# A fused attention and two-layer MLP kernel: all attention scores as float32 matmuls, with the two halves of the features in two row tiles of TensorE

## The chip, the cores and the metric

The kernel runs on one core of a Trainium2 chip, as one launch. The metric is the device time of one execution in microseconds. The engines are named as in the profile: PE is the matrix engine (its weight loads are listed apart, as PEld), DVE the vector engine, ACT the scalar engine, POOL is hardly used here, and SP issues the DMAs.

## The reference

Attention over 4 batches, 8 heads, 768 tokens and 64 features a head, in chunks of 32 tokens that see 16 tokens to the left, 8 to the right and 8 memory tokens; then two layers of an MLP, 512 to 2048 to 512, over all 3072 tokens.

```python
for c in range(nc):                      # 24 chunks of 32 tokens
    l_start = max(0, c_start - left_ctx)
    r_end = min(S, c_end + right_ctx)
    k_full = np.concatenate([mem_k, k[:, :, l_start:r_end]], axis=2)
    v_full = np.concatenate([mem_v, v[:, :, l_start:r_end]], axis=2)
    scores = scale * np.matmul(q_c, k_full.transpose(0, 1, 3, 2))
    scores = scores - np.max(scores, axis=-1, keepdims=True)
    a = np.exp(scores)
    a = a / (np.sum(a, axis=-1, keepdims=True) + 1e-09)
    out[:, :, c_start:c_end] = np.matmul(a, v_full)
...
h = x @ w_in                             # layer 1
x = (h * np.clip(h + 3.0, 0.0, 6.0) / 6.0) @ w_out
...
h = x @ w_in                             # layer 2
g = np.where(h >= 1, h, np.where(h <= -1, 0.0, (h + 1) ** 2 / 4.0))
x = g @ w_out
```

## The kernel before

**Attention.** The tokens are cut into 32 blocks of 96 queries (`QB`) and 128 keys (`KB`). A block has two halves of four heads (`GRP`): half 0 has its 64 features a head on partitions 0 to 63, half 1 on 64 to 127. Each call of `group(j, half, key)` does one half of block `j`: scores (tile `sc`), a maximum over keys, `exps` on ACT (tile `st`), `weigh` and `norm` on DVE, `turn` (four transposes on PE into `tp`), a copy `pt` on ACT or DVE, `values` (four matmuls on PE into `pv`, heads in turn on output partitions 0 to 63 and 64 to 127), and `x_high`/`x_low`, which write the result as a sum of two rounded parts into the MLP's input tiles `xhi` and `xlo`.

**Two kinds of scores.** The first ten blocks (`NEARLY`) are "early": PE adds the mask with one bfloat16 matmul (L373) and the four heads' scores with float32 matmuls on 64 rows (L379). The other 22 blocks are "late": the loads bring each half's q and k twice, to both halves of the partitions; ACT and DVE split q and k into a rounded part and the rest (`qs` L407 and L415, `ks` L410 and L417); PE makes the scores with `fp32r` matmuls on all 128 rows (L424, two of 256 columns a run, two runs a half); and DVE adds the mask and the two parts in two steps (L430, L436).

**MLP.** `xbuf` holds 6 tiles `n` of 512 tokens a layer. For each of 16 slices `f` of the hidden features (step `k` counts them over both layers, 192 in all) PE makes `ph` (12 matmuls, L526 to L528), ACT and DVE the activation and its two parts `ghi` and `glo`, and PE adds 12 matmuls into four PSUM tiles `py` (layer 1, L575 to L577) or `po` (layer 2, L580 to L582). After 16 slices ACT or DVE copy them out to `ysb` or `osb` and SP stores them. Layer 2 loads layer 1's result back as `x2raw`. The weights come packed and are unpacked by ACT and DVE (`raw`, `w`), once a layer.

**What sets the order.** `Plan.run` is a list scheduler that runs when the program is built. Each task has an engine (or two to choose from), an estimated duration, a key (a due time in steps of `k`) and buffers; a buffer takes a slot of a pool when its first task starts, and gives it back after the last. Each engine's instructions are emitted in the order of planned starts, so on the chip every engine works through a fixed list. The pools of interest: PSUM banks `a` (2; scores, `tp` and `pv` of attention), `y` (4) and `h` (2); places `o` (2) for results to be stored, `in` (2) for q and k, `lv` (3) for v, `st` (2), `pt` (1). In the first blocks some of these may also take `w` or `y` slots. Where PE would stand idle in the first 60 us of the plan, matmuls on a zero tile `warm` are put in (L687).

Blocks 0 to 5 feed the first tile `n = 0` and come ahead of the MLP; block order is all first halves, then all second halves. The other blocks are spread over the MLP steps of layer 1 by their keys.

Of the kernel before, what the change touches and what calls it, by code (L numbers as in the profile page):

```python
# [75 lines left out]
class Plan:  # L76
# [41 lines left out]
    def slot_for(self, b):  # L118

        found = []  # L120
        for p in b.pools:
            free = [s for s in self.pools[p] if not s.used]
            if len(free) > b.keep.get(p, 0):
                found.append(min(free, key=lambda s: s.at))
        return min(found, key=lambda s: s.at) if found else None

    def run(self, at):
# [13 lines left out]
        while left:  # L141
            best = None
            for e, ts in ready.items():
                found = []
                blocked = set()
                for t in sorted(ts, key=lambda t: (t.key, t.n)) if e == "SP" else ts:
                    est = max(free[e], t.ready)
                    for b in t.bufs:
                        if b.slot is None:
                            s = None if blocked & set(b.pools) else self.slot_for(b)  # L150
                            if s is None:
                                est = None
                                break
                            est = max(est, s.at + HOP)
                    if est is None and e == "SP":

                        blocked.update(p for b in t.bufs if b.slot is None for p in b.pools)
                    if est is not None:
                        found.append((est, t))
# [18 lines left out]
            if t.kb:  # L178
                bw = max(bw, t.end + 1500) + t.kb / 0.39
                t.end = bw  # L180
            for b in t.bufs:
                if b.slot is None:
                    b.slot = self.slot_for(b)
                    b.slot.used = True
# [31 lines left out]
def fused_kernel(ctx: ExitStack, tc: tile.TileContext, qkv, qk, vv, wpk, const, out):  # L216
# [4 lines left out]
        "w": NSLOT, "xhi": 2, "xlo": 2, "r": 2, "ghi": 3, "glo": 3, "st": 2, "pt": 1, "xt": 1,  # L221
        "o": 2, "in": 2, "lv": 3, "qs": 1, "ks": 1, "sm": 4,
# [107 lines left out]
    q_buf, v_buf = {}, {}  # L330

    def early_load(j, key):
        q = q_buf[j] = Buf(["w", "in"], [128, NP * (QB + KB)], F32, "q_sb", w=1)
        v = v_buf[j] = Buf(["w", "in"], [128, H * D], F32, "v_sb", w=1)
        o = NP * (QB + KB)
        add(("SP", 400), key - 6, lambda e: nc.sync.dma_start(tile_of(q), qkv[j, :, :o]), writes=[(q, 0)], kb=448)
        add(("SP", 400), key - 4, lambda e: nc.sync.dma_start(tile_of(v), qkv[j, :, o:]), writes=[(v, 0)], kb=256)

    def group(j, half, key):
        early = j < NEARLY  # L340
        first = key < 0
        bank = ["a", "y"] if first else ["a"]
        spare = ["w"] if first else []
        st = Buf(["st"] + spare, [128, GRP, KB], F32, "st", w=4)
        sm = Buf(["sm"], [128, 4, GRP], F32, "sm")
        pt = Buf(["pt"] + spare, [128, GRP, QB], F32, "pt", w=4)
        tp = Buf(bank, [128, GRP, QB], F32, "tp")
        pv = Buf(bank, [128, 2, QB], F32, "pv")
        small = lambda i: tile_of(sm)[:QB, i]

        def exps(src, n):
            s = tile_of(st)[:QB]
            for i in range(n):
                A.activation(
                    out=s[:, i, :], in_=src[:, i, :], func=AF.Exp, scale=scale,
                    bias=small(2)[:, i:i + 1], accum_out=small(0)[:, i:i + 1],
                )

        def peak(e, src):
            V.tensor_reduce(out=small(1), in_=src(), axis=AX.X, op=ALU.max)  # L360

        def negate(e):
            V.tensor_scalar(out=small(2), in0=small(1), scalar1=-scale, scalar2=None, op0=ALU.mult)

        if early:
            sc = Buf(bank, [128, GRP, KB], F32, "sc", a=1)
            q = q_buf[j]

            def scores(e):
                t, c = tile_of(q), tile_of(sc)  # L370
                q3 = t[:, :NP * QB].rearrange("p (a t) -> p a t", a=NP)
                k3 = t[:, NP * QB:].rearrange("p (a t) -> p a t", a=NP)
                P.matmul(  # L373
                    c[:QB], cbf[:QB, 3 * KB:3 * KB + QB], mask_of(j, GRP),
                    start=True, stop=False, skip_group_check=True,
                )
                hp = 64 * half
                for i in range(GRP):
                    P.matmul(  # L379
                        c[:QB, i, :], q3[hp:hp + 64, i, :], k3[hp:hp + 64, i, :],  # L380
                        start=False, stop=True, skip_group_check=True,
                    )

            add(("PE", 1350), key - 4, scores, [(q, 0), "cbf"], [(sc, 0)], hold=[st], line="scores")
            src, at = lambda: tile_of(sc)[:QB], (sc, 0)
            add(("DVE", dve(512, psum=True)), key - 3.5, lambda e: peak(e, src), [at], [(sm, 1)])
            add(("DVE", 90), key - 3.4, negate, [(sm, 1)], [(sm, 2)])
            add(("ACT", 1420), key - 3, lambda e: exps(src(), GRP), [at, (sm, 2)], [(st, 0), (sm, 0)])
        else:

            over = key > 1.75 * NF
            x = Buf(["in", "w"] if over else ["in"], [128, LATE_W], F32, "late_sb")
            xv = Buf(["lv"], [128, GRP * D], F32, "late_v")
            qs = Buf(["qs"], [128, GRP, QB], F32R, "qs")
            ks = Buf(["ks"], [128, GRP, 2, KB], F32R, "ks")
            g = 2 * (j - NEARLY) + half
            q3 = lambda: tile_of(x)[:, :GRP * QB].rearrange("p (a t) -> p a t", a=GRP)
            k3 = lambda: tile_of(x)[:, GRP * QB:LATE_W].rearrange("p (a t) -> p a t", a=GRP)

            def load(e, hp):  # L400
                nc.sync.dma_start(tile_of(x)[hp:hp + 64], qk[g])

            def load_v(e):
                nc.sync.dma_start(tile_of(xv), vv[g])
# [7 lines left out]
            add(("SP", 350), key - 9, lambda e: load(e, 0), writes=[(x, 0)], kb=224, after=last_w if over else (), line="load")  # L412
# [345 lines left out]
```

## Time and profile before

| | us |
|---|---|
| median of 3 runs (lowest, highest) | 1214.09 (1213.93, 1215.21) |
| the profiled execution: its time | 1214.17 |
| the profiled execution: span from the first to the last instruction | 1212.4 |
| PE busy in the span | 1194.1 |
| DVE busy | 747.5 |
| ACT busy | 555.1 |

The span is what the views of the trace divide up; 1.8 us of the execution's time lie around it. Matmuls are pipelined, and the profile's duration of one is longer than the distance to the next: how long a matmul takes of PE's time is read from the distance between starts. A float32 matmul is recorded as two instructions (a run of four matmuls is listed as x8).

### The profile page before, as it was taken

The numbers are of one execution on the slowest core, as the hardware profiler recorded it, in microseconds if no ns is written. First come the engines' busy times: TensorE is split into PE (matmuls) and PEld (weight loads), VectorE is DVE, ScalarE is ACT, GpSimd is POOL, SyncE is SP. The second block draws the span as 40 slices with busy tenths as digits, with TensorE's granted clock in tenths as the row PEclk, the third lists the DMA queues.
The fourth block names the chain that finished last, engine by engine and source line by source line (L and its number), as shares of the span: only waits on it lengthen the run. The fifth ranks groups of instructions, "written<-read, shape, count | busy, mean of one in ns | idle before, by whom it ended". The sixth has DMA issues, their size and how long they took to land.

```text
span 1212.4 us, 15631 instructions
## 1 busy us (share of the span) xinstructions
PE 1194.1 (98%) x5811; PEld 956.7 (79%) x5811; DVE 747.5 (62%) x1427; ACT 555.1 (46%) x1323; POOL 0.2 (0%) x4
## 2 busy tenths in 40 slices
PE   9999999999999999999999899999999999999998
PEld 6677777777777777777888688888888888888886
DVE  4999988768766764873598843533533533533433
ACT  4988656546545544653477722322222322322221
POOL 0000000000000000000000000000000000000000
PEclk9999999999999999999999999999999999999999
DMA  9615124223221320320255610200200200000000
GB/s 366 264 62 156 51 73 111 59 60 109 64 60 53 100 59 25 109 60 21 88 181 184 193 34 1 71 1 1 70 1 1 70 1 1 35 1 1 35 1 35
DMA packets 36060, 86.74 MB, mean 72 GB/s; under 512 B 4624, under 2 KB 10384, under 8 KB 35984
## 3 DMA queue, kind: packets, MB, share of 16 engines
q1 hardware_dynamic: 35984, 85.74, 22.2%
q8 instruction: 46, 0.75, 0.3%
q14 instruction: 30, 0.25, 0.1%
HBM read 73.14 MB, written 12.58 MB: 71 GB/s over the span
## 4 chain that ended last, share of the span: by engine, by line
PE 79%; DVE 10%; ACT 5%; DMA 4%; issue 1%; SPq 0%; ACTq 0%; DVEq 0%
PE ph L526 12%; PE ph L527 12%; PE ph L528 12%; PE po L580 7%; PE po L581 7%; PE po L582 7%; PE py L575 5%; PE py L576 5%; PE py L577 5%; DMA raw<-wpk 2%; PE pv L467 2%; PE sc L379 1%; PE tp L457 1%; PE sc L424 1%; DVE raw L297 1%
## 5 line engine op out<-in xcount | busy, mean ns | idle before, releaser
L526 PE MATMUL ph<-xhi,w 128*128 128x512 f32 x768 | 303.9, 396 | 0.3 <-DVE r L552 0.3
L527 PE MATMUL ph<-xlo,w 128*128 128x512 f32 x768 | 299.5, 390 | 0.0
L528 PE MATMUL ph<-xhi,w 128*128 128x512 f32 x768 | 299.4, 390 | 0.0
L549 ACT ACTIVATE r<-r,bias 128x512 f32<-128x512 f32 x96 | 69.4, 723 | 288.3 <-DVE r L546 288.3
L556 DVE TENSOR_TENSOR glo<-r,ghi 128x512 fp32r<-128x512 f32 x192 | 132.2, 689 | 81.3 <-ACT ghi L555 80.2
L555 ACT CAST ghi<-r 128x512 fp32r<-128x512 f32 x192 | 119.3, 622 | 116.6 <-DVE r L552 71.6
L526 PEld LDWEIGHTS ph<-xhi,w 128*128 128x128 f32 x768 | 144.2, 188 | 31.3 <-DVE r L552 0.7
L528 PEld LDWEIGHTS ph<-xhi,w 128*128 128x128 f32 x768 | 144.2, 188 | 30.9
L527 PEld LDWEIGHTS ph<-xlo,w 128*128 128x128 f32 x768 | 144.3, 188 | 27.7
L546 DVE TENSOR_SCALAR r<-ph 128x512 f32<-128x512 f32 x96 | 66.3, 691 | 148.3 <-PE ph L528 148.3
L575 PE MATMUL py<-ghi,w 128*128 128x512 f32 x384 | 157.2, 409 | 0.5 <-ACT ysb L597 0.4
L580 PE MATMUL po<-w,ghi 128*128 128x512 f32 x384 | 149.7, 390 | 4.3 <-DVE ysb L601 2.3
L576 PE MATMUL py<-glo,w 128*128 128x512 f32 x384 | 150.4, 392 | 0.0
L577 PE MATMUL py<-ghi,w 128*128 128x512 f32 x384 | 150.2, 391 | 0.0
L581 PE MATMUL po<-w,ghi 128*128 128x512 f32 x384 | 149.4, 389 | 0.0
L582 PE MATMUL po<-w,glo 128*128 128x512 f32 x384 | 149.4, 389 | 0.0
L552 DVE TENSOR_TENSOR r<-ph,r 128x512 f32<-128x512 f32 x96 | 66.3, 691 | 75.9 <-ACT r L549 75.9
L539 ACT ACTIVATE r<-ph,bias 128x512 f32<-128x512 f32 x96 | 65.7, 684 | 90.3 <-PE ph L528 78.9
L542 DVE SCALAR_TENSOR_TENSOR r<-r,ph 128x512 f32<-128x512 f32 x96 | 65.4, 681 | 46.8 <-ACT r L539 46.0
L580 PEld LDWEIGHTS po<-w,ghi 128*128 128x128 f32 x384 | 72.0, 188 | 20.4 <-ACT ysb L597 2.9
L575 PEld LDWEIGHTS py<-ghi,w 128*128 128x128 f32 x384 | 72.1, 188 | 17.2 <-ACT ysb L597 1.4
L577 PEld LDWEIGHTS py<-ghi,w 128*128 128x128 f32 x384 | 72.1, 188 | 16.2
(66 smaller groups left out, 1331.2 us busy)
## 6 DMA issues: line engine op xcount, KB each, us to landing
raw<-wpk SPq DMA_DIRECT2D x64, 512.0 KB, 4.3
late_sb<-qk SPq DMA_DIRECT2D x88, 224.0 KB, 3.5
ymid<-ysb SPq DMA_DIRECT2D x24, 256.0 KB, 2.9
x2raw<-ymid SPq DMA_DIRECT2D x24, 256.0 KB, 4.3
out<-osb SPq DMA_DIRECT2D x24, 256.0 KB, 2.0
late_v<-vv SPq DMA_DIRECT2D x44, 128.0 KB, 2.1
q_sb<-qkv SPq DMA_DIRECT2D x10, 448.0 KB, 7.0
v_sb<-qkv SPq DMA_DIRECT2D x10, 256.0 KB, 6.8
```

What stands on the lines that cost most here:

```text
L526: P.matmul(p, whi[:, c, :], xh[:, c, :], start=(c == 0), stop=False)
L527: P.matmul(p, whi[:, c, :], xl[:, c, :], start=False, stop=False)
L528: P.matmul(p, wlo[:, c, :], xh[:, c, :], start=False, stop=(c == NC - 1))
L549: add(("ACT", act(T) + 100), k + 0.35, lambda e: A.activation(out=rt(), in_=rt(), func=AF.Square, bias=bias[:, 1:2], scale=0.5,), [], [(r, ...
L555: add(("ACT", act(T)), k + 0.5, lambda e: A.copy(tile_of(ghi), rt()), [(r, 0)], [(ghi, 0)])
L556: add(("DVE", dve(T)), k + 0.6, lambda e: V.tensor_tensor(out=tile_of(glo), in0=rt(), in1=tile_of(ghi), op=ALU.subtract,), [(r, 0), (ghi, ...
L575: P.matmul(y, w2hi, gh, start=first, stop=False)
L576: P.matmul(y, w2hi, gl, start=False, stop=False)
L577: P.matmul(y, w2lo, gh, start=False, stop=last)
L580: P.matmul(y, gh[:, t], wt[:, 0], start=first, stop=False)
L581: P.matmul(y, gh[:, t], wt[:, 1], start=False, stop=False)
L582: P.matmul(y, gl[:, t], wt[:, 0], start=False, stop=last)
```

## The change

- The block's two halves are one task on PE: `scores` of a block alternates between half 0 (rows 0 to 63 of the array) and half 1 (rows 64 to 127), each with its own PSUM bank. From block 6 on (from the second tile on) both halves' `turn` is one run of eight transposes, and both halves' `values` one run of eight matmuls.
- All blocks use the float32 scores. Early blocks keep the mask by PE; for the late ones DVE adds the mask in one step of 512 columns. The splits of q and k, and their second loads, are gone.
- Keys: the first tile's blocks come block by block (both halves next to each other) rather than half by half.
- Pools: `st` 3, `pt` 2, `lv` 2 (of twice the width), `qs` and `ks` gone. Results to be stored may also take `st` and `in` places in layer 2 and for the last tile of layer 1.
- The planner reckons 1900 rather than 1500 ns for a DMA's latency, takes all slots of a task at once, and fills 1300 ns more with `warm` matmuls ahead of the first real one.

```diff
-        "w": NSLOT, "xhi": 2, "xlo": 2, "r": 2, "ghi": 3, "glo": 3, "st": 2, "pt": 1, "xt": 1,
-        "o": 2, "in": 2, "lv": 3, "qs": 1, "ks": 1, "sm": 4,
+        "w": NSLOT, "xhi": 2, "xlo": 2, "r": 2, "ghi": 3, "glo": 3, "st": 3, "pt": 2, "xt": 1,
+        "o": 2, "in": 2, "lv": 2, "sm": 4,
...
+        for half in range(2):
+            g, p, c = 2 * (j - NEARLY) + half, slice(64 * half, 64 * half + 64), slice(256 * half, 256 * half + 256)
+            add(
+                ("SP", 350), key - 9, lambda e, g=g, p=p: nc.sync.dma_start(tile_of(q)[p], qk[g]),
+                writes=[(q, half)], kb=224, after=last_w if over else (), line="load",
+            )
...
-            def q_low(e):
-                V.tensor_tensor(out=tile_of(qs)[64:], in0=q3()[64:], in1=tile_of(qs)[64:], op=ALU.subtract)
-
-            def k_low(e):
-                V.tensor_tensor(out=tile_of(ks)[:, :, 1], in0=k3(), in1=tile_of(ks)[:, :, 0], op=ALU.subtract)
...
+            for i in range(GRP):
+                for h in half:
+                    P.matmul(
+                        tile_of(sc[h])[:QB, i, :], q3[64 * h:64 * h + 64, i, :], k3[64 * h:64 * h + 64, i, :],
+                        start=not by_pe and i == 0, stop=True, skip_group_check=True,
                     )
...
+            def mask(e):
+                V.tensor_tensor(out=s(), in0=tile_of(sc[h])[:QB], in1=mask_of(j, GRP), op=ALU.add)
...
+        add(
+            ("PE", 1200 + 460 * by_pe), keys[0] - 4, scores, [(q, 0), (q, 1), "cbf"],
+            [(sc[0], 0), (sc[1], 0)], hold=st, line="scores",
+        )
...
+            add(
+                ("PE", 710), keys[1] - 2, lambda e: [turn(h) for h in half], [(st[0], 0), (st[1], 0), "ident"],
+                [(tp[0], 0), (tp[1], 0)], hold=pt, line="turn",
+            )
...
-                o = Buf(["o"], [128, T], F32, "osb" if l else "ysb")
+
+                o = Buf(["o", "st", "in"] if l or n == NT - 1 else ["o"], [128, T], F32, "osb" if l else "ysb")
...
-                    while at + ns <= t.start:
+                    while at + ns <= t.start + more:
```

Three places show how the instructions move.

PE, between two MLP steps of layer 1, with a late block under way. Before (`sc` are a half's scores, `ph` and `py` the MLP's):

```order
L528 MATMUL ph<-xhi,w 128x512
L424 MATMUL sc<-ks,qs 96x256 x2
L575 MATMUL py<-ghi,w 128x512
L576 MATMUL py<-glo,w 128x512
L577 MATMUL py<-ghi,w 128x512
L575 MATMUL py<-ghi,w 128x512
L576 MATMUL py<-glo,w 128x512
L577 MATMUL py<-ghi,w 128x512
L424 MATMUL sc<-ks,qs 96x256 x2
```

and of the change (`tp` are the transposes of one block, `sc` the scores of the next):

```order
L520 MATMUL ph<-xhi,w 128x512
L393 MATMUL tp<-ident,st 128x96 x8
L567 MATMUL py<-ghi,w 128x512
L568 MATMUL py<-glo,w 128x512
L569 MATMUL py<-ghi,w 128x512
L567 MATMUL py<-ghi,w 128x512
L568 MATMUL py<-glo,w 128x512
L569 MATMUL py<-ghi,w 128x512
L386 MATMUL sc<-q_sb 96x128 x8
L567 MATMUL py<-ghi,w 128x512
```

Eight short runs of attention a block (four of scores, two of transposes, two of values) have become three longer ones, and six MLP matmuls stand between a block's transposes and the next block's scores.

PE at the start of the program, behind the first `warm` matmuls. Before, one half of blocks 0, 1 and 2:

```order
L373 LDWEIGHTS cbf
L373 MATMUL sc<-cbf 96x512
L379 MATMUL sc<-q_sb 96x128 x4
L373 LDWEIGHTS cbf
L373 MATMUL sc<-cbf 96x512
L379 MATMUL sc<-q_sb 96x128 x4
L687 LDWEIGHTS warm
L687 MATMUL sc<-warm 128x512
```

and of the change, both halves of block 0, and the masks of block 1:

```order
L379 LDWEIGHTS cbf
L379 MATMUL sc<-cbf 96x512
L379 LDWEIGHTS cbf
L379 MATMUL sc<-cbf 96x512
L386 MATMUL sc<-q_sb 96x128 x8
L379 LDWEIGHTS cbf
L379 MATMUL sc<-cbf 96x512
```

Both masks now go ahead of the block's eight float32 matmuls.

ACT where layer 2 begins, around the copies `ysb` of layer 1's last tile (`xhi<-x2raw` is layer 2's second input tile). Before:

```order
L555 CAST ghi<-r 128x512
L252 CAST xhi<-x2raw 128x512 x3
L252 CAST w<-raw 128x512
L281 ACTIVATE raw<-raw 128x512
L549 ACTIVATE r<-r,bias 128x512
L287 ACTIVATE raw<-raw 128x512
L555 CAST ghi<-r 128x512
L597 ACTIVATE ysb<-py 128x512 x2
```

and of the change:

```order
L547 CAST ghi<-r 128x512
L253 CAST w<-raw 128x512
L253 CAST xhi<-x2raw 128x512 x3
L253 CAST w<-raw 128x512
L590 ACTIVATE ysb<-py 128x512
L541 ACTIVATE r<-r,bias 128x512
L282 ACTIVATE raw<-raw 128x512
L590 ACTIVATE ysb<-py 128x512
```

ACT's first copy stands nearer behind the three casts of `x2raw`; the casts still stand ahead of it.

## Rows read from the trace of the kernel before

**Rows 1.** The page: busy us of each engine, share of the span, instructions.
```profile
PE 1194.1 (98%) x5811; PEld 956.7 (79%) x5811; DVE 747.5 (62%) x1427; ACT 555.1 (46%) x1323; POOL 0.2 (0%) x4
```

**Rows 2.** Windows: stretch, us, busy us (count) of PE, PEld, DVE, ACT, POOL; clock, DMA.
```profile
10.00:20.00 10.00, 10.00 (x42) 7.01 (x42) 5.94 (x17) 2.98 (x16) 0.00 (x0) 1.00 1.03 409
20.00:30.00 10.00, 10.00 (x76) 7.78 (x75) 6.84 (x19) 6.91 (x31) 0.00 (x0) 1.00 1.02 404
...
60.00:100.00 40.00, 39.33 (x218) 29.67 (x216) 37.84 (x74) 32.08 (x79) 0.00 (x0) 1.00 0.31 106
...
200.00:550.00 350.00, 347.61 (x1831) 274.12 (x1830) 246.92 (x547) 182.75 (x531) 0.00 (x0) 1.00 0.26 71
...
650.00:700.00 50.00, 45.35 (x197) 36.33 (x196) 44.53 (x72) 37.18 (x62) 0.00 (x0) 1.00 0.58 189
```

**Rows 3.** Windows of the instructions on tile w alone: PE's are the MLP matmuls.
```profile
200.00:550.00 350.00, 318.43 (x1269) 228.89 (x1268) 0.00 (x0) 0.00 (x0) 1.00 0.26 71
700.00:1200.00 500.00, 500.00 (x2208) 414.02 (x2207) 0.68 (x1) 0.00 (x0) 1.00 0.05 18
```

**Rows 4.** Timeline of PE in layer 1: start us, us, instruction.
```profile
255.65 0.40 PE L424 MATMUL sc<-ks,qs 128*96 128x256 f32 x2
255.88 0.39 PE L575 MATMUL py<-ghi,w 128*128 128x512 f32 x1
...
258.65 0.39 PE L577 MATMUL py<-ghi,w 128*128 128x512 f32 x1
258.96 0.55 PE L467 MATMUL pv<-pt,late_v 128*64 128x96 f32 x8
259.45 0.50 PE L526 MATMUL ph<-xhi,w 128*128 128x512 f32 x1
259.79 0.40 PE L527 MATMUL ph<-xlo,w 128*128 128x512 f32 x1
```

**Rows 5.** Timeline of PE in the first 60 us.
```profile
17.77 2.02 PE L379 MATMUL sc<-q_sb 64*96 64x128 f32 x8
19.72 1.54 PE L467 MATMUL pv<-pt,v_sb 128*64 128x96 f32 x16
21.20 0.90 PE L457 MATMUL tp<-ident,st 96*128 96x96 f32 x4
...
24.41 0.91 PE L467 MATMUL pv<-pt,v_sb 128*64 128x96 f32 x8
25.25 0.50 PE L687 MATMUL tp<-warm 128*128 128x384 bf16 x1
...
57.76 1.11 PE L379 MATMUL sc<-q_sb 64*96 64x128 f32 x8
58.80 0.55 PE L467 MATMUL pv<-pt,v_sb 128*64 128x96 f32 x8
```

**Rows 6.** Timeline of ACT at the start; in brackets its idle time before, and what ended it.
```profile
20.67 0.32 ACT L252 CAST xhi<-pv 128x192 fp32r<-128x192 f32 x1 [4.68 <-PE pv L467]
```

**Rows 7.** PE's waits where layer 2 begins (640 to 730 us): us, times, longest.
```profile
PE po L580 <- DVE ysb L601: 2.3, 1, 2.3
PE po L580 <- ACT ysb L597: 2.1, 2, 1.7
```

**Rows 8.** Timeline at the end.
```profile
1205.18 1.37 DVE L599 COPY osb<-po 128x512 f32<-128x512 f32 x2 [2.46 <-PE po L582]
...
1206.79 0.39 PE L582 MATMUL po<-w,glo 128*128 128x512 f32 x1
1208.12 1.29 DVE L599 COPY osb<-po 128x512 f32<-128x512 f32 x2 [1.57 <-DMA out<-osb]
```

**Rows 9.** Groups of instructions, 200 to 550 us, by form: busy us, mean ns.
```profile
L430 DVE TENSOR_TENSOR st<-sc,cbf 96x256 f32<-96x256 f32 x70 | 29.2, 417 | 22.2 <-PE sc L424 21.7
...
L410 DVE TENSOR_TENSOR ks<-late_sb,ks 128x512 fp32r<-128x512 f32 x35 | 24.1, 688 | 0.7
...
L252 ACT COPY pt<-tp 128x384 f32<-128x384 f32 x23 | 11.0, 476 | 5.5 <-PE tp L457 5.5
```

More of the change, by code (lines that the diff above doesn't have):

```diff
@@ L116, in add, with slots_for @@
         return t
[L118 to L125, printed above, removed]
+    def slots_for(self, t):
+        taken = []
+        for b in t.bufs:
+            if b.slot is None:
+                found = []
+                for p in b.pools:
+                    free = [s for s in self.pools[p] if not s.used and s not in taken]
+                    if len(free) > b.keep.get(p, 0):
+                        found.append(min(free, key=lambda s: s.at))
+                if not found:
+                    return None
+                taken.append(min(found, key=lambda s: s.at))
+        return taken
     def run(self, at):
@@ L330, in fused_kernel @@
     q_buf, v_buf = {}, {}
[L332 to L339, printed above, removed]
-        early = j < NEARLY
-        first = key < 0
+    WQ = NP * (QB + KB)
@@ L342, in group, with block @@
+    def block(j, keys):
+        first = keys[1] < 0
         bank = ["a", "y"] if first else ["a"]
         spare = ["w"] if first else []
[L344 to L378, printed above, removed]
+        by_pe = j < NEARLY
@@ new lines, in block, with scores @@
+        q, v = q_buf[j], v_buf[j]
+        half = range(2)
+        of = lambda pools, shape, name, **keep: [Buf(pools, shape, F32, name, **keep) for _ in half]
+        sc = of(bank, [128, GRP, KB], "sc")
+        st = of(["st"] + spare, [128, GRP, KB], "st", w=4)
+        sm = of(["sm"], [128, 4, GRP], "sm")
+        pt = of(["pt"] + spare, [128, GRP, QB], "pt", w=4)
+        tp = of(bank, [128, GRP, QB], "tp")
+        pv = of(bank, [128, 2, QB], "pv")
+        def scores(e):
+            t = tile_of(q)
+            q3 = t[:, :NP * QB].rearrange("p (a t) -> p a t", a=NP)
+            k3 = t[:, NP * QB:].rearrange("p (a t) -> p a t", a=NP)
+            if by_pe:
+                for h in half:
@@ new lines, in block @@
+        add(
+            ("PE", 1200 + 460 * by_pe), keys[0] - 4, scores, [(q, 0), (q, 1), "cbf"],
+            [(sc[0], 0), (sc[1], 0)], hold=st, line="scores",
+        )
+        for h in half:
+            softmax(h, keys[h])
+        if first:
+            for h in half:
+                add(("PE", 380), keys[h] - 2, lambda e, h=h: turn(h), [(st[h], 0), "ident"], [(tp[h], 0)], hold=[pt[h]], line="turn")
+                copy(h, keys[h])
+                add(("PE", 560), keys[h] - 1, lambda e, h=h: values(h), [(pt[h], 0), (v, h)], [(pv[h], 0)], line="values")
+        else:
+            add(
+                ("PE", 710), keys[1] - 2, lambda e: [turn(h) for h in half], [(st[0], 0), (st[1], 0), "ident"],
+                [(tp[0], 0), (tp[1], 0)], hold=pt, line="turn",
+            )
+            for h in half:
+                copy(h, keys[1])
+            add(
+                ("PE", 1050), keys[1] - 1, lambda e: [values(h) for h in half],
+                [(pt[0], 0), (pt[1], 0), (v, 0), (v, 1)], [(pv[0], 0), (pv[1], 0)], line="values",
+            )
@@ L509, in fused_kernel @@
+        for h in half:
+            result(h, keys[h])
     ybuf = {}
@@ L672, in fused_kernel @@
         order = plan.run({"PE": 1000, "DVE": 1000, "ACT": 2200, "POOL": 1000, "SP": 700})
-        at = 1000
+        at, more = 1000, 1300
         for t in order:
@@ L691, in fused_kernel @@
                         at += ns
-                at = t.start + dict(t.ways)["PE"]
+                at, more = t.start + dict(t.ways)["PE"], 0
             t.emit(t.eng)
```

218 lines of the change are left out of this document (92 added, 126 removed).

## The prediction

> **What bounds the kernel now.** I read the page's busy line first: PE is busy for 1194.1 us [rows 1], so a change must take time from PE, or from the stretches where PE waits or does filler. The windows tell these apart [rows 2]. From 10 to 30 us PE is full, but of the slow kind: the run of eight score instructions that takes 1.04 us at 57.76 (to the next start) takes 1.95 us at 17.77 [rows 5]. The clock is listed as 1.00 there, but a factor of nearly two is that between the levels of 2.4 and 1.2 GHz. ACT is busy for 2.98 and 6.91 of these two stretches of 10 us: it waits for PE's results, as the row with 4.68 us behind `values` shows [rows 6]. From 60 to 100 us DVE is busy for 37.84 of 40 us and PE's matmuls wait for unpacked weights and softmax. From 200 to 550 us PE is busy for 347.61 of 350 us while DVE has 246.92: PE alone is the bound. From 650 to 700 us PE has 45.35 of 50: waits where layer 2 begins. Layer 2 is matmuls without a gap, 2208 in 500 us, 0.2264 us each [rows 3]; nothing in the change shortens that.
>
> **What a late block costs PE.** From 200 to 550 us PE does 1269 MLP matmuls [rows 3], at 0.2264 us 287.3 us, and 1831 - 1269 = 562 attention instructions [rows 2, 3]. A late block has 8 of scores, 8 of transposes and 16 of values, so this is 17.6 blocks, and the 350 us leave (350 - 287.3)/17.6 = 3.56 us a block. Of these the scores are four runs of 0.23 us (255.65 to 255.88), 0.92. A run of values costs 0.08 (the matmul before it takes 0.31 rather than 0.23), 0.49 for itself and 0.11 (the matmul behind takes 0.34) [rows 4]: 0.68, two a block 1.36. The other 1.28 us are the two runs of transposes, MLP matmuls that come a little slower behind each run, and waits (2.4 us of the 350, 0.14 a block).
>
> **Scores of a late block.** Now four `fp32r` runs on the whole array; then one run of 16 float32 instructions that alternate between two row tiles. The nearest row in kind is one half's run in one row tile, 1.04 us at full clock [rows 5]. If the second tile's instructions run beside the first's, the block's run takes that again; if not, 2.08 us. Between these I take 1.04, since `values` already alternates between two tiles (of columns): at low clock sixteen such instructions take 1.48 us and eight 0.84 [rows 5], so eight more take 0.64, 0.08 each for 96 columns, where an instruction of the scores, in one tile, takes 1.95/8 = 0.24 for 128. Per column that is 0.8 against 1.9 ns, as it must be if two run at a time. With a change of tiling at both ends as for `values`, 0.08 + 0.11, the run costs 1.23, against 0.92: **+0.31 us a block**.
>
> The Trainium skill (TensorEngine Tiling (Array Packing), Tiling Modes, Key Properties) says that a change of tiling mode drains the engine, which speaks against this change: the scores of before needed no such change. Rows 4 agree, with 0.08 ahead of a run and 0.11 behind it; without the drain the sum would be 22 x 0.19 = 4.2 us lower.
>
> **Values and transposes.** Two runs of values become one: 0.68 plus eight more instructions, 0.64 at low clock, half of that at full clock, 0.33: 1.01 against 1.36, **-0.35**. The rest, 1.28 us, goes partly with the number of runs, which falls from eight to three. Bounds: 0 (it is all transposes, which stay) and -0.5 (the slow matmuls and waits, about half of it, fall by 5/8, and some drain). I take the middle, **-0.25**.
>
> Sum for a late block: 0.31 - 0.35 - 0.25 = -0.29, for 22 blocks **-6.4 us**, between -1 and -12.
>
> **DVE, ACT and DMA.** A half loses on DVE a split of k (0.688), one of q, and four mask steps of 0.42 for one of twice the columns [rows 9], over 1.6 us; ACT loses two casts; SP loses half of the q and k loads. From 200 to 550 us this is hidden behind PE, and so priced at nothing. It would count only where DVE ends last, up to 100 us, and there all but one or two blocks are early ones, whose work on DVE and ACT stays.
>
> **The start.** The six blocks of the first tile need on PE, at low clock, two runs of 1.95 us each; side by side one run does. That takes some 2 us a block from the stretch of 10 to 30 us in which ACT stands idle for 20 - 2.98 - 6.91 = 10.1 us [rows 2]. From then on ACT and DVE have the same weights to unpack and the same softmax, so they end earlier by the idle time saved: at most 10.1, and nothing where the added filler eats it (a rival below). I take **-4**: nearer to 0, as the first result comes later than now (both masks and more `warm` matmuls are ahead of it), the DMAs are full (409 GB/s), and `warm` matmuls between transposes and values still stand in PE's list.
>
> **Where layer 2 begins.** PE waits 2.3 us for DVE's and 2.1 us for ACT's copies of `ysb` [rows 7]. The second wait is for a place: the store of an earlier copy must land first. With `st` and `in` places it goes. The first is not for a place: its copy follows DVE's other work without a gap, and the casts of `x2raw` still stand ahead of the copies. **-2**, between 0 and -4.4.
>
> **The end.** The third `osb` copy waits 1.57 us for a store and the last pair ends at 1209.41. With free places the last copy, which starts 0.6 us into the pair, about 1208.7, can start once the last matmul is done, 1206.79 + 0.39 = 1207.2 [rows 8]. **-1.4**.
>
> **Sum.** -6.4 - 4 - 2 - 1.4 = -13.8 us, on the profiled execution's 1214.17: **1200.4 us**. (The median of the runs is 0.1 lower, which makes no odds.) A measurement of this kernel can tell about 0.2%, 2.4 us, from no change.
>
> **Rivals.**
>
> *The row tiles run one after the other* (slower). The block's scores take 2.08 us: 22 x 1.04 = 22.9 us more, and the start's 4 us go: 1227. For it: no row has two row tiles at a time. Against: the column tiles of `values`. It is slower than before from 0.45 us a block lost to imperfect pairing. Chance 0.06.
>
> *They pair only in part*: halfway, 1.56 us a run, 22 x 0.52 = 11.4 more: 1212, no change. Chance 0.08. The Trainium skill (TensorE: Matmul & The Clock Gate, Part 3, Measured speedup vs the span model) has 3.07 for four row tiles. An estimate from it, a quarter lost, would make the run about 1.35 us and the time some 7 us longer than my sum; no run here shows it yet.
>
> *Waits for the two `a` banks.* Scores, transposes and values of a block now each need both banks. Six MLP matmuls, 1.36 us, stand between transposes and the next scores; in that time two copies `pt` (0.476 each on ACT) must be through. If ACT has them one after the other behind another instruction, PE waits. At 0.63 us a block the gain is gone; at 1 us it is 22 us, 1222. Against: such waits are 0.14 us a block now, and DVE and ACT have less to do. Chance 0.08.
>
> *The start gets longer by 4 us instead of shorter*, since twice as many `warm` matmuls stand in PE's list: 1208. Chance 0.07.
>
> *The start gains the whole 10 and layer 2's waits go whole*: 1192. Chance 0.11.
>
> My forecast has 0.60, by itself 1194 to 1207. The range, **1189 to 1211**, leaves out the first rival, the upper half of the second, most of the third and little below, some 0.18. Faster by over 0.2%: the forecast, the last two rivals and the mild part of the third, 0.82; within 0.2%: 0.07; slower: 0.11.
>
> **What the profile after would show.** Score runs of 16 instructions that last about 1.1 us between MLP matmuls, the two tiles' starts close together; values runs of 16, about 0.8 us; fewer than 3.4 us a block from 200 to 550 us; ACT busy for clearly more than 9.9 us from 10 to 30 us; the first step of the second tile (step 16) 4 to 10 us earlier; one wait of about 2 us at layer 2's begin; the last `osb` copy within a microsecond of the last matmul. Wrong would be score runs near 2 us, PE idle more than 3% from 200 to 550 us, or a start that shows more filler and the same pace.

## The result and the profile after

The changed kernel takes 1180.10 us (median of 4 runs, 1178.85 to 1181.29), the kernel before 1214.01 beside it: a ratio of 0.974 (95% interval 0.969 to 0.979). The forecast was 1200.4 with a range of 1189 to 1211: the direction is right, the size is not. The profiled execution takes 1178.85 us with a span of 1177.1, 35.3 us less than the span of before, where the sum had 13.8.

To read the numbers below: the 47 runs of the kernel before, those beside the experiments among them, fall in two groups, 18 at 1204.6 to 1208.2 us and 29 at 1211.7 to 1217.2 (its profile is of the second), and the changed kernel, whose four runs lie within 2.5 us, gains some 25 us against the first.

The busy line, which answers to [rows 1]:

```profile
PE 1169.6 (99%) x6072; PEld 949.4 (81%) x6072; DVE 653.7 (56%) x1204; ACT 504.9 (43%) x1238; POOL 0.2 (0%) x4
```

PE gives up 24.5 us of busy time, and 10.8 us in which it stood idle. The windows, in the columns of [rows 2], two short stretches added:

```profile
10.00:20.00 10.00, 9.99 (x119) 7.53 (x116) 9.49 (x29) 9.09 (x46) 0.00 (x0) 1.00 1.03 406
20.00:30.00 10.00, 9.96 (x109) 7.35 (x108) 8.96 (x27) 10.00 (x43) 0.00 (x0) 1.00 1.03 405
...
120.00:130.00 10.00, 10.00 (x60) 8.02 (x59) 9.93 (x20) 6.18 (x18) 0.00 (x0) 1.00 0.09 26
...
140.00:150.00 10.00, 10.00 (x61) 8.13 (x60) 7.19 (x15) 5.54 (x17) 0.00 (x0) 1.00 0.05 14
200.00:550.00 350.00, 350.00 (x2014) 282.22 (x2014) 177.06 (x368) 144.88 (x457) 0.00 (x0) 1.00 0.15 45
650.00:700.00 50.00, 50.00 (x222) 41.42 (x221) 31.69 (x50) 22.61 (x38) 0.00 (x0) 1.00 0.27 85
```

and those of tile w alone, as in [rows 3]:

```profile
200.00:550.00 350.00, 312.05 (x1310) 241.51 (x1310) 0.00 (x0) 0.00 (x0) 1.00 0.15 45
```

ACT does 19.1 us of work from 10 to 30 us, where it did 9.9. From 200 to 550 us PE has no gap, and from 650 to 700 none either: neither wait of [rows 7] is left. A late block by the prediction's own count: 1310 MLP matmuls at 0.2264 us are 296.6; 2014 - 1310 = 704 attention instructions, 40 a block now (16 + 8 + 16), are 17.6 blocks; (350 - 296.6)/17.6 = **3.03 us, where before had 3.56**.

PE in layer 1, to be held against [rows 4], and at the start, against [rows 5]:

```profile
260.19 0.39 PE L520 MATMUL ph<-xhi,w 128*128 128x512 f32 x1
260.50 1.12 PE L386 MATMUL sc<-q_sb 64*96 64x128 f32 x16
261.55 0.50 PE L518 MATMUL ph<-xhi,w 128*128 128x512 f32 x1
261.89 0.40 PE L519 MATMUL ph<-xlo,w 128*128 128x512 f32 x1
...
265.58 0.39 PE L569 MATMUL py<-ghi,w 128*128 128x512 f32 x1
265.90 0.88 PE L399 MATMUL pv<-pt,v_sb 128*64 128x96 f32 x16
266.71 0.50 PE L518 MATMUL ph<-xhi,w 128*128 128x512 f32 x1
267.05 0.40 PE L519 MATMUL ph<-xlo,w 128*128 128x512 f32 x1
```

```profile
0.98 4.40 PE L673 MATMUL sc<-warm 128*128 128x512 bf16 x11 [0.98 <-DVE bias L655]
5.22 0.60 PE L379 MATMUL sc<-cbf 96*96 96x512 bf16 x2
5.75 1.12 PE L386 MATMUL sc<-q_sb 64*96 64x128 f32 x16
```

In layer 1 sixteen score instructions take 1.05 us to the next start (260.50 to 261.55), as eight did at full clock before: the two row tiles work side by side. Values take 0.81 (265.90 to 266.71). At the start a run of sixteen takes the same 1.05 us at 5.75 already (the next row starts at 6.80), where the runs of eight before took 1.95 until 25 us: PE is at its faster level (2.4 GHz, against 1.2) some 20 us earlier.

The end, with what [rows 8] show of before: the copies `osb` run one behind the other with no wait for a store.

```profile
1171.25 2.73 DVE L592 COPY osb<-po 128x512 f32<-128x512 f32 x4 [2.45 <-PE po L574]
```

Where the time went is seen from when a step begins, that is the first `ph` matmul of step `k` (each step has twelve), counted through the traces:

| start of, us | before | after | difference so far | gained since the line above |
|---|---|---|---|---|
| step 8 | 111.4 | 96.5 | -14.9 | 14.9 |
| step 16 | 162.2 | 149.5 | -12.7 | -2.2 |
| step 32 | 272.5 | 252.9 | -19.6 | 6.9 |
| step 80 | 586.5 | 558.4 | -28.1 | 8.5 |
| step 96 (layer 2) | 673.6 | 645.4 | -28.2 | 0.1 |
| step 104 | 722.9 | 688.9 | -34.0 | 5.8 |
| step 184 | 1158.1 | 1124.1 | -34.0 | 0 |
| end of the span | 1212.4 | 1177.1 | -35.3 | 1.3 |

From step 8 to 16 the changed kernel is slower, as PE does the scores of three blocks there, where before it did those of one and a half. So the start's gain is 14.9 us at step 8.

### The profile page after: what moved, and what is told of

It reads as the page before. It is cut to its first block, busy times and chain, and to the rows that moved or that the text cites. A ratio compares the mean times of both kernels' runs of the same rounds, so it can differ in the third digit from the quotient of the medians.

```text
span 1177.1 us, 15573 instructions
## 1 busy us (share of the span) xinstructions
PE 1169.6 (99%) x6072; PEld 949.4 (81%) x6072; DVE 653.7 (56%) x1204; ACT 504.9 (43%) x1238; POOL 0.2 (0%) x4
## 4 chain that ended last, share of the span: by engine, by line
PE 97%; ACT 1%; DVE 1%; DMA 1%; SPq 0%; issue 0%
PE ph L518 15%; PE ph L519 15%; PE ph L520 15%; PE py L567 8%; PE py L568 7%; PE py L569 7%; PE po L573 7%; PE po L574 7%; PE po L572 7%; PE sc L386 3%; PE pv L399 2%; PE tp L393 2%; DMA q_sb<-qkv 1%; PE pv L673 1%; ACT st L420 0%; PE tp L673 0%
## 5 line engine op out<-in xcount | busy, mean ns | idle before, releaser
L420 ACT ACTIVATE st<-st,sm 96x128 f32<-96x128 f32 x176 | 68.3, 390 | 52.0 <-DVE sm L416 51.9
```

## The experiments

Times are medians, to be held against the 1180.1 of the changed kernel or the two groups of before. "Span" and steps are of the profiled execution.

### The start: is it PE's level?

My theory: most of the 12.7 us ahead of step 16 come from PE reaching its faster level early, because the first run of `warm` matmuls is longer. The rival: row tiles side by side and the order by blocks. Two kernels take from the change's first run:

```diff
-        at, more = 1000, 1300
+        at, more = 1000, -4000      # x1: none ahead of the first masks
+        at, more = 1000, 0          # x2: 8 matmuls instead of 11
```

> The changed kernel without the run of warm matmuls ahead of the first masks and scores (it has 11 there; the result isn't touched). Theory: the start gained 12.7 us (step 16 at 149.5 us instead of 162.2) for the most part because those 11 matmuls, without a gap up to the masks and scores, bring PE to its faster level at about 5 us, where the kernel before stays at the lower one until about 27 us. Then this kernel's score runs take some 2 us each up to about 25 us, ACT is busy for clearly less than the 19.1 us that it has from 10 to 30 us, step 16 comes 4 to 10 us later (154 to 160 us), and the time is 1184 to 1190. Rival: the gain is that of the two row tiles side by side and of the new order of blocks. Then score runs of 16 take about 1.05 us all the same, or 2 us without harm, and the time is within 2 us of 1179.

> The changed kernel with the first run of warm matmuls as short as before (some 8 instead of 11); what follows it is still the two masks and the sixteen score instructions of both halves. Theory as for the run without them: what matters is that PE has enough work without a gap ahead of the first scores. If 8 and the masks still do it, the distance of starts falls from 0.43 to 0.22 us in them or right behind, and the time is 1178 to 1181; if not, score runs take 2 us up to some 25 us and the time is 1184 to 1190 as without any. Rival (tiles and order of blocks): within 2 us of 1179 and score runs of 2 us without harm.

Without any: 1181.44 us (1179.49 to 1182.22), step 16 at 152.3. With eight: 1179.61 (1179.19 to 1180.31), step 16 at 149.8. Both are within 1.5 us of the changed kernel; for the run without them the theory had 4 us or more. PE in that run:

```profile
4.71 2.03 PE L386 MATMUL sc<-q_sb 64*96 64x128 f32 x16 [0.77 <-DMA q_sb<-qkv]
...
10.65 2.03 PE L386 MATMUL sc<-q_sb 64*96 64x128 f32 x16
...
15.28 0.55 PE L399 MATMUL pv<-pt,v_sb 128*64 128x96 f32 x8
...
18.81 1.12 PE L386 MATMUL sc<-q_sb 64*96 64x128 f32 x16
```

Score runs take about 2 us up to 12.6 us, but values at 15.28 and the scores at 18.81 are at the faster level already. So the changed kernel gets there by itself 12 us earlier than before; what raises the level there isn't shown. The whole `warm` run is worth 2.8 us of span in it (1.3 by the medians), and its added length nothing that can be told: with eight matmuls the span is 0.3 longer. That is a miss of the theory as I had put it. It doesn't speak against the level as the cause in the kernel before, whose profile shows it at the lower one until 27 us. The third kernel is the kernel before with the longer first run alone:

```diff
-        at = 1000
+        at, more = 1000, 1300
...
-                    while at + ns <= t.start:
+                    while at + ns <= t.start + more:
...
-                at = t.start + dict(t.ways)["PE"]
+                at, more = t.start + dict(t.ways)["PE"], 0
```

> The kernel before with one thing of the change alone: the first run of warm matmuls 1300 ns longer (10 instead of 7). Theory: PE reaches its faster level at about 5 us, the eight score instructions at 17 us take 1.05 us instead of 1.95, ACT is busy for more than 15 of the 20 us from 10 to 30, and the time falls by 6 to 10 us, to 1204 to 1208. Rival (tiles and order of blocks): no change or up to 1.5 us more, 1213 to 1216. If PE doesn't get faster with the longer run either, because one half's scores leave a gap behind it, the time stays too, and the trace tells this from the rival by the score instructions' duration.

1206.56 us (1205.45 to 1208.44 in 10 runs), none of them in the second group of before; the ratio to all of before's runs is 0.997 (0.994 to 1.000), as these hold both groups. Against the profiled execution of before the span falls by 8.0, from 1212.4 to 1204.4, and all of it stands ahead of step 16 (162.2 to 154.0). PE there:

```profile
0.98 4.45 PE L687 MATMUL sc<-warm 128*128 128x512 bf16 x10 [0.98 <-DVE bias L669]
...
5.79 1.25 PE L379 MATMUL sc<-q_sb 64*96 64x128 f32 x8
```

The run of eight takes 1.17 us to the next start (6.96) instead of 1.95. As forecast by the theory: 8 us for the level alone, in the kernel before, against its second group of runs. Against the first group the longer run gains nothing. It also fills a gap, the 0.55 us for which PE waited for `q_sb` ahead of the first score run; whether the length or the filled gap raises the level isn't told apart.

To get a profile of the first group, the kernel before was run three more times.

> The kernel before again, for its profile. Its runs so far fall in two groups, 1204.6 to 1208.2 (18 of 50) and 1211.7 to 1217.2 (32), and its profile is of the second. Theory: the first group is the runs in which PE reaches its faster level early. If this run is of the first group, the score runs of eight at 6 to 25 us take 1.05 us, step 16 comes at 153 to 155 us, as with the longer warm run, and the rest of the trace is as before. Rival: the two groups differ elsewhere (loads, layer 2), and score runs take 1.95 us until 25 us in both. A run of the second group tells nothing new.

> As for the first look: if the time is 1204 to 1208.5, score runs of 1.05 us before 25 us and step 16 at 153 to 155 us by the theory, 1.95 us by the rival.

> As for the first look: if the time is 1204 to 1208.5, score runs of 1.05 us before 25 us and step 16 at 153 to 155 us by the theory, 1.95 us by the rival.

All three fell in the second group (1215.3, 1214.5, 1216.4; the 50 and 32 runs of the expectation count three runs of that group twice), so the first is still known by its times alone. But the first two are not like the profile of before either. PE in the first, and two of its windows:

```profile
6.60 1.11 PE L379 MATMUL sc<-q_sb 64*96 64x128 f32 x8
...
8.52 2.02 PE L379 MATMUL sc<-q_sb 64*96 64x128 f32 x8
```

```profile
0.00:10.00 10.00, 8.35 (x34) 4.62 (x35) 3.06 (x11) 4.14 (x17) 0.20 (x4) 0.89 0.80 278
10.00:20.00 10.00, 10.00 (x52) 7.24 (x50) 5.38 (x14) 3.11 (x18) 0.00 (x0) 0.50 1.03 409
```

PE was at the faster level for two runs of scores and then fell to the lower, with a granted clock of 0.50 from 10 to 20 us. So before stands on an edge: the same program reaches the level or not, keeps it or not. That its first group is the runs that keep it fits the time of the kernel with the longer first run, but no profile shows it. The Trainium skill (TensorE: Matmul & The Clock Gate, What's actually happening) says that the low rate is the default and that activity releases it, and that when this comes can vary from run to run. The profiles agree that it varies: PE's first rise comes at 4.4 and 4.0 us in the first two of these runs, at 29.9 in the third and at 27.0 in the profile of before. That activity doesn't raise it at once [rows 2] show, with PE busy for 10.00 of 10 us from 10 to 20 us, still at the lower level.

The filler behind the first scores was one of the prediction's rivals (it was to make the start longer by 4 us). It was taken out:

```diff
-            if t.eng == "PE" and t.start <= FILL:
+            if t.eng == "PE" and t.start <= 6000:
```

> The changed kernel with warm matmuls only ahead of the first masks and scores (11 of its 164); from there to 60 us PE has its own work and waits where the others stood. Theory: the filler keeps PE without gaps, and with it the faster level; without it PE waits for softmax and weights in gaps of 1 us and more, score runs take 2 us again in places between 10 and 45 us, step 16 comes 2 to 8 us later, and the time is 1181 to 1187. Rival (one of the prediction's: more filler in PE's list delays work): PE gets through the same list sooner, step 16 comes 1 to 3 us earlier, 1176 to 1178. If the first 60 us are set by ACT's and DVE's unpacking and the level doesn't matter there, within 1.5 us of 1180.

1182.35 us (1181.60 to 1182.55), step 16 at 153.1.

```profile
24.74 0.87 PE L393 MATMUL tp<-ident,st 96*128 96x96 f32 x4 [1.30 <-DVE st L431]
...
26.40 2.02 PE L386 MATMUL sc<-q_sb 64*96 64x128 f32 x16
```

```profile
20.00:30.00 10.00, 7.20 (x62) 4.99 (x57) 7.89 (x22) 8.54 (x32) 0.00 (x0) 0.69 1.03 406
```

Without filler PE waits for softmax, falls to the lower level at about 24 us (0.69 granted from 20 to 30 us), and score runs take 2 us there. The filler doesn't delay; it is worth 2.2 us by the medians. The rival falls.

The order of the first tile's softmax by blocks, put back to halves:

```diff
-                i - m - 1.0 if n == 0 else ... for i in (i, i + 1)
+                i // 2 + h * (m // 2) - m - 1.0 if n == 0 else ... for h in range(2)
```

> The changed kernel with the softmax keys of the first tile's six blocks in the old order, all first halves ahead of all second halves, where the change goes block by block. Theory: the start's gain is the clock (8 us by the kernel before with the longer first run) and DVE's relief between steps 8 and 20 (6 us by the run with DVE load), not the order: within 2 us of 1180. Rival: the order by blocks frees places and banks sooner; without it step 16 comes 3 to 6 us later, 1183 to 1186.

1181.06 us (1179.96 to 1182.31): as the theory has it, the order is worth no more than a measurement can tell. (Its level falls once, granted 0.83 from 50 to 60 us, where that of the changed kernel holds.)

### Scores in two row tiles

```diff
-            for i in range(GRP):
-                for h in half:
+            for h in half:
+                for i in range(GRP):
```

> The changed kernel with each block's scores in another order: the eight instructions of half 0, then the eight of half 1, where the change alternates; the number of instructions and everything else is the same. Theory: the gain on late blocks rests on two row tiles at work at a time, which needs neighbours in different tiles. Then a run of sixteen takes 1.9 to 2.1 us instead of 1.05, from 200 to 550 us a block costs 0.85 to 1.0 us more, 22 late blocks 18 to 22 us, and the start 1 to 4 us: 1197 to 1205. Rival: the engine's order doesn't matter, or a run waits for something else: 1178 to 1181.

1193.20 us (1192.64 to 1193.68), 13.1 more: the order matters, as the theory says, but by less than its 17.

```profile
305.17 1.63 PE L386 MATMUL sc<-q_sb 64*96 64x128 f32 x16
306.73 0.50 PE L567 MATMUL py<-ghi,w 128*128 128x512 f32 x1
```

A run takes 1.56 us, not 2.08: also in turn the tiles overlap by half a run. From 200 to 550 us a block costs 3.55, +0.52. So the alternation carries 0.51 us a run of the 1.04 that two tiles can save, and the rest comes without it. At the start this half of the pairing is worth 4.0 us by step 8 (100.5) and 5.0 by step 16 (154.5).

### Runs joined

The late blocks' transposes and values in separate runs for each half:

```diff
-        if first:
+        if True:
             for h in half:
                 add(("PE", 380), keys[h] - 2, lambda e, h=h: turn(h), ...
```

> The changed kernel with the transposes and the values of the late blocks in separate runs for each half again, as all kernels have them in the first tile; the scores stay in one run. Theory: the part of the gain that I called the rest (0.5 us a late block, where I had 0.25) comes with the number of runs, since each run of another tiling costs some 0.2 us at its two ends. Then a block costs 0.35 us more for values (two runs of 0.68 for one of 1.01) and 0.08 to 0.17 more for transposes: from 200 to 550 us 3.45 to 3.55 us a block, and with 22 blocks 9.5 to 11.5 us: 1189 to 1192. Rival: the rest is DVE's relief, and runs of transposes cost nothing at their ends: only the 0.35, 7.7 us: 1187 to 1188.5.

1193.23 us (1192.10 to 1194.02). The windows, all instructions and those of tile w, and PE around two of the short runs:

```profile
200.00:550.00 350.00, 350.00 (x1967) 273.56 (x1966) 181.77 (x386) 137.09 (x432) 0.00 (x0) 1.00 0.15 45
```

```profile
200.00:550.00 350.00, 314.45 (x1271) 231.75 (x1270) 0.00 (x0) 0.00 (x0) 1.00 0.15 45
```

```profile
256.77 0.55 PE L399 MATMUL pv<-pt,v_sb 128*64 128x96 f32 x8
257.25 0.50 PE L567 MATMUL py<-ghi,w 128*128 128x512 f32 x1
257.60 0.40 PE L568 MATMUL py<-glo,w 128*128 128x512 f32 x1
...
258.07 0.49 PE L393 MATMUL tp<-ident,st 96*128 96x96 f32 x4
258.35 0.48 PE L567 MATMUL py<-ghi,w 128*128 128x512 f32 x1
258.66 0.40 PE L568 MATMUL py<-glo,w 128*128 128x512 f32 x1
```

1271 x 0.2264 = 287.8; 696/40 = 17.4 blocks; (350 - 287.8)/17.4 = 3.58 us a block. That is the 3.56 of before. So joining the runs gives 0.55 us a block, the whole gain of the late blocks, and everything else in them (new scores, lighter DVE, waits gone) sums to 0.02. With each run that is joined to another goes a slow matmul behind it, 0.35 us behind values (257.25 to 257.60) and 0.31 behind transposes (258.35 to 258.66) where 0.23 is the pace, and a little on some ten matmuls further on. The time is 1 us beyond the theory's range, as step 16 is also 2.1 us later; PE's level falls once on the way (granted 0.83 from 50 to 60 us).

### DVE's relief

Three idle DVE operations a half in the late blocks give back most of what the change took off (57 of 70 us from 200 to 550 us):

```diff
+                for d in (4.9, 4.85, 4.8):
+                    add(("DVE", dve(512)), key - d, extra, [(q, 0), (q, 1)], [])
```

> The changed kernel with three idle DVE operations of 512 columns added to each half of a late block, about as much DVE work (some 2 us a half) as the change took off there; their results are used by nothing. Theory: from 200 to 550 us PE is the bound, DVE's work is hidden, and the gain comes with fewer runs: a block stays at 3.0 to 3.1 us, PE waits for less than 1 us, and the time is 1179 to 1182. Rival: the missing half of the rest (waits of 2.4 us in that stretch, and slow matmuls far behind a run) was DVE's relief: 3.2 to 3.3 us a block, PE waits of 2 us or more, and 1184 to 1187.

1186.05 us (1185.60 to 1188.48), 6.0 more: the rival's time, but not its place.

```profile
120.00:130.00 10.00, 6.87 (x34) 5.07 (x35) 9.90 (x20) 5.23 (x15) 0.00 (x0) 0.84 0.09 28
...
200.00:550.00 350.00, 350.00 (x2013) 282.22 (x2012) 234.19 (x458) 144.93 (x458) 0.00 (x0) 1.00 0.15 45
```

```profile
PE ph L524 <- DVE r L540: 3.7, 2, 3.1
```

From 200 to 550 us nothing changes although DVE has 57 us more: 3.05 us a block, no wait. The price is paid between step 8 (96.3 us, after: 96.5) and step 18 (168.5, after: 162.2): PE waits 3.7 us there for DVE's `r`, and the granted clock from 120 to 130 us is 0.84. The span is 6.4 longer, and the whole of it stands at step 32 (259.3 instead of 252.9). DVE's relief is worth some 6 us, all of it in the stretch in which DVE is still full (9.93 of 10 us at 120 to 130 in the changed kernel, 7.19 at 140 to 150). Part of it is the lower level, as 0.84 shows. In the kernel before, DVE is nearly full for longer, up to 200 us:

```profile
140.00:150.00 10.00, 9.71 (x51) 7.48 (x50) 9.96 (x20) 5.79 (x12) 0.00 (x0) 1.00 0.22 61
...
180.00:190.00 10.00, 9.83 (x60) 7.61 (x61) 9.30 (x22) 6.62 (x19) 0.00 (x0) 1.00 0.58 170
```

But PE itself waits for only 2.4 us there from step 8 to 20. So 6 us is what the load costs the changed kernel, which comes to step 8 some 15 us sooner; it isn't a share of the 35.3 us.

### Where layer 2 begins, and the end

Places for results as before; and, in another kernel, the planner's latency of a load as before:

```diff
-                o = Buf(["o", "st", "in"] if l or n == NT - 1 else ["o"], [128, T], F32, ...   # x6
+                o = Buf(["o"], [128, T], F32, ...
-                bw = max(bw, t.end + 1900) + t.kb / 0.39                                       # x11
+                bw = max(bw, t.end + 1500) + t.kb / 0.39
```

> The changed kernel with results in the two o places alone, as before. Theory: of the 5.8 us gained where layer 2 begins (step 96 to 104 in 43.5 instead of 49.3 us) the 4.4 us of waits for ysb copies, and the 1.4 us at the end, come from the added places: PE waits 2 to 4.4 us again at layer 2's begin, the end takes 5.2 us again, and the time is 1183.5 to 1186.5. Rival: at layer 2's begin it was DVE's and ACT's lighter work that let the copies come in time, and the places only shorten the end: no waits there, 1181 to 1182.

1186.01 us (1184.62 to 1186.40), in the theory's range, but in part by luck. Step 96 to 104 takes 47.6 us instead of 43.5, the end (from step 184) 54.5 instead of 53.0. Another 1.8 us, which have nothing to do with the theory, stand ahead of step 16, and 1.6 of them between steps 0 and 4. PE waits 2.29 us for DVE's `r` there, and its level falls behind it; in the changed kernel PE waits 2.30 us at the same place, and its level holds (granted 1.00). Of the waits at layer 2 only those for ACT's copies are back, 1.9 us; most of the rest of the 4.1 is PE's level:

```profile
665.27 0.50 PE L572 MATMUL po<-w,ghi 128*128 128x512 f32 x1 [1.25 <-ACT ysb L590]
...
666.29 0.63 PE L518 MATMUL ph<-xhi,w 128*128 128x512 f32 x1
666.71 0.63 PE L519 MATMUL ph<-xlo,w 128*128 128x512 f32 x1
```

```profile
50.00:60.00 10.00, 7.71 (x33) 4.69 (x29) 9.43 (x19) 8.79 (x27) 0.00 (x0) 0.83 1.03 405
...
660.00:670.00 10.00, 8.11 (x28) 5.91 (x27) 8.66 (x14) 6.90 (x12) 0.00 (x0) 0.83 0.75 194
```

Behind the wait of 1.25 us the matmuls come every 0.42 us (666.29 to 666.71) instead of 0.23, and the granted clock of that window is 0.83, as in the one at the start.

> The changed kernel with the planner's old estimate of a load's latency, 1500 instead of 1900; it only shifts the planned starts and so the order of instructions. Theory: no term of the sum rests on it: 1178.5 to 1181.5. Rival: orders that fit the loads less well cost waits in the first 60 us, where the DMAs are full: 1182 to 1186.

1184.71 us (1183.38 to 1187.00): the rival's time, but not at the start (step 16 at 150.1). Step 96 to 104 takes 49.7 us, +6.2. DVE there, and PE:

```profile
660.74 0.43 DVE L253 CAST xhi<-x2raw 128x512 fp32r<-128x512 f32 x1 [0.84 <-DMA x2raw<-ymid]
...
664.09 1.28 DVE L594 TENSOR_SCALAR ysb<-py 128x512 f32<-128x512 f32 x2
```

```profile
664.92 0.47 PE L572 MATMUL po<-w,ghi 128*128 128x512 f32 x1 [1.96 <-DVE ysb L594]
```

With the shorter latency the planner gives DVE a cast of `x2raw` whose load hasn't landed; DVE stands 0.84 us, the `ysb` copies behind it come late, and PE waits 1.96; another 2.5 us are two waits for DVE's `r` ahead of it (653.16 and 659.95), and 0.6 one for an `ysb` of ACT. In the changed kernel that cast isn't on DVE's list here, and the copies come in time. So places and latency are both needed there. The same two were put into the kernel before with the longer `warm` run, first the places alone, then both:

> The kernel before with two things of the change, the longer first run of warm matmuls (1206.6 us by itself) and the added places for layer 1's last and layer 2's results. Theory: the places alone take the waits where layer 2 begins: 1.4 us at the end and 4 to 5.8 at the begin: 1199 to 1201.5. Rival: the first of those waits, 2.3 us for DVE's copy, is DVE's own order of work and stays: 1.4 and some 2 us: 1202.5 to 1204.

> The kernel before with three things of the change: the longer first run of warm matmuls, the added places, and the planner's latency of 1900 for a load (the first two alone: 1202.8 us, with step 96 to 104 in 48.1 us). Theory: at layer 2's begin the two belong together: with the old latency the planner puts a cast of x2raw where its load hasn't landed, DVE waits 1 us for it with the ysb copies behind it, and PE 2 us; with 1900 the cast stands later. So the wait goes here too, step 96 to 104 takes 43.5 to 45 us, and the time is 1197 to 1200. Rival: it is DVE's and ACT's relief from late blocks that makes the begin of layer 2 free, and a new latency only shuffles the order: 1201 to 1205, with 2 us or more of waits for ysb or w.

Places alone: 1202.80 us (1201.59 to 1204.11), the rival's range, step 96 to 104 in 48.1 instead of 49.6. PE still waits, and its level falls (granted 0.83 from 680 to 690 us):

```profile
PE po L580 <- ACT w L252: 2.0, 1, 2.0
```

With the latency too: 1202.41 us (1202.06 to 1203.12; ratio to before 0.991, 0.988 to 0.994).

```profile
650.00:700.00 50.00, 50.00 (x222) 41.44 (x221) 43.67 (x74) 33.07 (x56) 0.00 (x0) 1.00 0.53 168
```

Where layer 2 begins the theory holds: no wait, 43.5 us, as in the changed kernel, although DVE and ACT have the old load. The time missed its range all the same: against the places alone the new order loses 1.9 us between steps 16 and 80 (426.0 instead of 424.1, with 2.5 us of waits of `tp` for DVE's `xlo` where there were 0.7), 0.8 ahead of step 16 and 1.1 from step 184 on.

## Why the prediction was wrong

Right were the direction, the pairing of the row tiles (a run with its ends costs 0.08 + 1.05 + 0.11 = 1.24 us; 1.23 was said), values in one run (1.01, as said) and the end (-1.3; -1.4 was said, though its own rows, 1208.7 and 1207.2, give 1.5). No wait for the `a` banks shows from step 16 on. The steps that failed, by size:

**The start** (-4 said, -14.9 at step 8, -12.7 at step 16). It took PE's lower level until 25 us as given, and the additional `warm` matmuls as a delay alone, even a rival of 1208. The rows had the level in plain sight: 1.95 against 1.04 us for the same run. By the kernel before with the longer first run the level alone is 8.0 us, all of it by step 8 (103.4); the changed kernel gets to it by the longer run or without. The reason given for the -4, the pairing of the score runs, holds: losing half of it costs 4.0 by step 8. What the other 2.9 us are stays open. The bound of 10.1, ACT's idle time from 10 to 30 us, is too low by 4.8 at step 8, where no late block's DVE work counts yet (96.3 with the idle load).

**DVE, ACT and DMA** (nothing said). I had written that a lighter DVE would count only up to 100 us, where few late blocks are. [rows 2] stop at 100 us and go on at 200, and no row of the stretch between was shown: DVE is nearly full there up to 200 us in the kernel before (over 9 of each 10 us, but for 150 to 160) and up to some 145 in the changed kernel, with the first late blocks in it. The idle load costs the changed kernel some 6 us, between steps 8 and 18; from 200 us on it is nothing, as said.

**Late blocks** (-0.29 a block said, -0.53 measured; 22 blocks, -11.7, at the edge of the bounds). Joining the runs had -0.35 and -0.25, in sum -0.60, and gives 0.55. The mis-sized term is the scores: +0.31 against 0.92 us for four runs, taken from one row of 0.23. Over the 71 runs from 200 to 550 us a run of before takes 0.267 to the next start, 1.07 a block, and waits of 0.14 a block go; what was to cost 0.31 nets to nothing.

**Where layer 2 begins** (-2 said, bound -4.4, measured -5.8). "The first is not for a place: its copy follows DVE's other work without a gap" was read from the copy and the rows just ahead of it. The gap was 4 us earlier on DVE, behind a load; and the one line that cures it, the planner's latency, I had costed at nothing without a word. Only places and latency together free the stretch. DVE in the kernel before:

```profile
686.01 0.43 DVE L252 CAST xhi<-x2raw 128x512 fp32r<-128x512 f32 x1 [1.15 <-DMA x2raw<-ymid]
...
689.37 1.28 DVE L601 TENSOR_SCALAR ysb<-py 128x512 f32<-128x512 f32 x2
```

By the table the 35.3 us are 14.9 up to step 8, 4.7 from there to step 32, 8.6 to step 96, 5.8 to step 104 and 1.3 at the end. The parts that experiments price (8.0 for the level, 4.0 for half of the pairing at the start, 6.4 for DVE's load, 11.7 for late blocks, 5.8, 1.3) come from different kernels, overlap and can't be added: their sum is 37.2. Left open too is what sets the two groups of the kernel before.

Of the rivals none came. The nearest is "the start gains the whole 10 and layer 2's waits go whole", 1192, which had two of the right places and some 60% of the size. The Trainium skill (TensorEngine Tiling (Array Packing), Tiling Modes, Key Properties) says that a change of tiling mode drains the engine, which I had weighed against the new scores. The traces agree in that runs in another tiling cost time at their ends (0.34 instead of 0.23 us for the matmul behind `values`); that this is a drain they don't show. For the change it told the other way: one run of values and one of transposes fewer are 0.55 us a block, more than the scores' new ends cost.

## What to carry to other kernels

If the same instruction takes twice as long in one stretch as in another, price the way out of the slower level, not only the work in it: a few filler matmuls ahead of the first real ones were worth 8 us of a kernel that got there by itself only at 27 us, and little in one that got there sooner. Relief on an engine is worth what it is in the stretch where that engine is full, so look for the end of that stretch in ten-microsecond windows before it is priced at nothing. And a late copy is followed back along its own engine's list until a gap shows, since the cure (here an estimate of a load's latency) is where the gap is.

## Not expected of the hardware

- A column "1.00" for PE's granted clock doesn't show the level ahead of its first change: [rows 2] list it from 10 to 30 us, where instructions take twice their time, and another profiled run of the same kernel lists 0.50 from 10 to 20 us with the same durations. The trace of before has no record of the clock ahead of 27.0 us.
- Row tiles in turn, not alternated, still overlap: 1.56 us for two runs of eight, where one takes 1.04.
- A wait of 1.25 us in layer 2 was followed by matmuls 0.42 us apart (granted 0.83), but the waits of [rows 7], 2.3 us and up to 1.7, were followed by none (granted 1.00 in [rows 2]). In the three more runs of the same kernel PE waited there too, 2.0 us at most at a time, and its level fell each time (granted 0.66, 0.83 and 0.66 from 690 to 700 us). So the length of one wait doesn't tell whether the level falls.
